# First expert by blocks of 128 tokens, its weights and rows gathered in another order, and narrow counting products in the first search

## The chip, the core and the metric

The kernel runs on one core of one Trainium2 chip. A core has five engines that run side by side and wait for each other through semaphores: TensorE (PE in the profile, its weight loads PEld), VectorE (DVE), ScalarE (ACT), GpSimd (POOL) and SyncE (SP), and DMA engines that move data between the chip's main memory (HBM), SBUF and, by way of the engines, PSUM. The metric is the device time of one execution in microseconds (us), as the median of several runs.

## The reference

The first half is a gated linear attention with a complex decay, the second a mixture of experts with a fixed capacity. Cut to what matters here:

```python
# attention -> x of 3072 tokens by 384 features
logits = x @ w_gate                      # 3072 x 8
order = np.argsort(-logits.flatten())
for idx in order:                        # greedy: best pair first
    tok, e = int(idx) // E, int(idx) % E
    if assigned[tok] >= 0 or counts[e] >= cap:   # cap = 3072 // 8 = 384
        continue
    assigned[tok] = e
    counts[e] += 1
for e in range(E):
    mask = assigned == e
    h = np.maximum(x[mask] @ w1[e], 0.0)         # 384 x 384 by 384 x 1024
    out[mask] = h @ w2[e]                        # 384 x 1024 by 1024 x 384
```

## The kernel before

The attention takes the first 252 us or so and is the same in both kernels. It leaves the rows `x` in HBM (`xd`) and the logits of all tokens in SBUF (`z.lg`, 128 partitions by 24 columns by 8 experts).

**The search.** `Router.find` finds which expert fills up next and at which logit. It narrows a threshold in five rounds. In each round VectorE compares all tokens with 32 candidate thresholds (`ind`, 128 x 24 x 32), TensorE counts the hits by expert (`cnt`, from `ind` and the one-hot choice `oh`), VectorE turns the counts into a flag `f`, and TensorE adds the chosen step to the threshold row `thr` in PSUM: once with `steps` (called S below) and once with `weight` and `fm` (called FM). S and FM write `thr`, which the comparison reads, so a round goes round the engines: compare, count, reduce, FM, compare. The count is made by six products, each of four token columns at once, so that a result lies in four diagonal blocks. For most experts VectorE adds the four blocks (`merge`: `cs` and `half`); for the first search (`BY_PE`) ScalarE copies the block to SBUF (`y`) and four more products against an identity add them (`gather`, tile `sm`). In the first search the comparison is made in two halves (`PARTS`).

When the search has closed (a product `cnt<-f,onesb`, called CLOSE below, and a product with `tri`, the running count over partitions), `eidx` names the rows of the expert's weights, and `Router.slots` works out which tokens go in which slot: VectorE makes one-hot tiles `o` and `rh`, six products give `cnt<-rh,o`, and four small operations write the row numbers `idx`.

**The gathers.** GpSimd issues indirect DMAs, all on one queue: `w1t` (one expert's w1, 1.57 MB), `w2t` (1.57 MB) and three of `xg` (128 token rows each, 0.2 MB). For experts in `W2_LATE` the rows go ahead of w2.

**The expert.** Rows are transposed on TensorE (`acc<-ident,xg`, nine 128 x 128), then come 24 products per w1 (8 column blocks by 3) and 24 per w2 (3 row blocks by 8). Experts 1 to 7 use split numbers: ScalarE rounds a tile to a high part (`w1h`, `w2h`, `xh`, `hh`), VectorE makes the low part (`w1l`, `w2l`, `xl`, `hl`), and each product is three fp32r matmuls of 384 columns: 144 per expert. Expert 0 (`WHOLE1`, `WHOLE2`) uses plain fp32, where a matmul shows as two records in the trace, and needs no split. For all experts the tokens are 384 columns wide, so the first product wants all three row blocks.

**The order.** Nothing is issued as the code is written. `experts` records every operation in a `Plan`; `rank` gives each a due time minus an offset by kind (the table `M_OFF`), and `in_order` (a list scheduler with fixed costs) writes out one static order for each engine. Each engine then runs its own list strictly in that order. The main products of expert e and the search for expert e+1 are interleaved in this way. Ahead of expert 0's first transpose TensorE runs `WARM` products of two constants (`acc<-ident,mask`).

## Time and profile before

| | us |
|---|---|
| median of 3 runs (545.6 to 547.11) | 545.8 |
| the profiled execution | 550.18 |
| its span, first to last instruction | 548.4 |
| PE busy / DVE busy in the span | 445.6 / 437.1 |
| first search: count of round 1 to CLOSE | 257.7 to 269.2 |
| first main product of expert 0 (w1) | 288.0 |
| CLOSE of the second search | 295.4 |
| last matmul | 540.5 |

The profiled execution took 550.18 us, 1.8 us more than its span and 4.4 us more than the median of the runs shown; differences within the span are read as differences of the median. Positions are in us from the start of the span. A "record" is one matmul instruction of the trace; matmuls overlap in the pipe, so the pitch between records, not the length of one, is what they cost.

### The profile page before, as it was taken

Reading aid. Unit: us, or ns where it says so; the run is one execution under the profiler, and the core shown is the slowest. Engines: PE = TensorE matmul, PEld = TensorE weight load, DVE = VectorE, ACT = ScalarE, POOL = GpSimd, SP = SyncE. Lnnn points to the kernel's source line nnn. Section 1 sums busy time; section 2 is a strip of 40 time slices with the busy share of each in tenths; the row PEclk is TensorE's granted clock in tenths of the full one; section 3 lists DMA queues with packets and bytes.
Section 4 is the critical chain, followed back from the end, with each engine's and each line's share of the span. In section 5 each row is a group of like instructions: output and inputs, shape, how many; then the busy total and the mean of one; then the engine's idle time right before and its main releaser. Section 6 shows DMA issues by size and latency. Waiting matters only on the chain. (4 is left out here: it accounts for less than half of the span.)

```text
span 548.4 us, 9215 instructions
## 1 busy us (share of the span) xinstructions
PE 445.6 (81%) x3383; PEld 392.6 (72%) x3383; DVE 437.1 (80%) x1267; ACT 276.5 (50%) x422; POOL 72.9 (13%) x87
## 2 busy tenths in 40 slices
PE   0005997699679967995489899999999999999994
PEld 0005996599678856994375458887889888999993
DVE  7999999979899989944667768889899898965240
ACT  5997579828887688322012513244172432834231
POOL 1000000000000000000121311332132223460102
PEclk9999999579859995998569999999999999999999
DMA  8625867578756885541071513245062431950001
GB/s 240 234 76 140 240 200 240 140 193 215 247 155 178 242 276 154 136 120 45 0 274 48 208 47 131 78 177 221 30 244 73 159 130 39 393 189 16 30 14 43
DMA packets 47596, 82.47 MB, mean 150 GB/s; under 512 B 5568, under 2 KB 43200, under 8 KB 45504
## 3 DMA queue, kind: packets, MB, share of 16 engines
q1 hardware_dynamic: 38720, 42.57, 27.2%
q0 software_dynamic: 5376, 34.61, 16.9%
q10 hardware_dynamic: 3456, 4.72, 2.5%
q8 instruction: 26, 0.43, 0.3%
q14 instruction: 18, 0.15, 0.1%
HBM read 53.49 MB, written 9.44 MB: 115 GB/s over the span
## 5 line engine op out<-in xcount | busy, mean ns | idle before, releaser
L131 PE MATMUL sc<-KQ 96*128 96x128 f32 x384 | 60.3, 317 | 41.6 <-DMA KQ<-f 40.7
L131 PEld LDWEIGHTS sc<-KQ 96*128 96x128 f32 x384 | 55.2, 226 | 44.0 <-DMA KQ<-f 41.6
L131 ACT ACTIVATE hh<-acc 128x384 fp32r<-128x384 f32 (+1 forms) x64 | 30.6, 490 | 75.2 <-PE acc L131 75.0
L131 PE MATMUL acc<-w2h,hl 128*128 128x384 f32 x168 | 55.1, 346 | 0.0
L131 PE MATMUL acc<-w2l,hh 128*128 128x384 f32 x168 | 54.9, 345 | 0.0
L131 PE MATMUL acc<-w2h,hh 128*128 128x384 f32 x168 | 54.4, 343 | 0.0
L131 PE MATMUL acc<-xh,w1h 128*128 128x384 f32 x168 | 53.6, 347 | 0.3 <-DVE idx L131 0.2
L131 PE MATMUL acc<-xl,w1h 128*128 128x384 f32 x168 | 53.1, 345 | 0.0
L131 PE MATMUL acc<-xh,w1l 128*128 128x384 f32 x168 | 52.6, 343 | 0.0
L131 POOL DMA_INDIRECT w1t<-in_w,eidx x8 | 8.8, 1099 | 312.4 <-DVE of L131 269.3
L131 ACT ACTIVATE ot<-acc 128x384 f32<-128x384 f32 x24 | 11.8, 492 | 70.7 <-PE acc L131 55.8
L131 DVE TENSOR_TENSOR f<-kq,CS 128x768 f32<-128x768 f32 x48 | 43.7, 949 | 0.9 <-ACT CS L131 0.9
L131 DVE SCALAR_TENSOR_TENSOR hl<-acc,hh 128x384 fp32r<-128x384 f32 x56 | 30.4, 551 | 15.9 <-ACT hh L131 15.3
L131 PE MATMUL y<-am,V 128*64 128x128 f32 x384 | 38.0, 288 | 3.0 <-DVE am L131 2.0
L131 DVE TENSOR_TENSOR ind<-m,thr 128x768 bf16<-128x768 f32 (+1 forms) x40 | 33.7, 849 | 6.9 <-PE thr L131 6.6
L131 PE MATMUL kp<-ident,KQ 96*128 96x96 f32 x160 | 25.0, 301 | 15.7 <-DMA KQ<-f 9.5
L131 POOL DMA_INDIRECT out<-ot,idx x24 | 25.3, 1053 | 93.2 <-ACT ot L131 82.9
L131 DVE TENSOR_TENSOR am<-sc,mask 128x512 f32<-128x512 f32 x48 | 31.5, 680 | 6.2 <-PE sc L131 6.1
L131 PE MATMUL U<-V,kt 128*96 128x96 f32 x320 | 35.2, 270 | 0.9 <-DVE tmp L131 0.9
L131 POOL DMA_INDIRECT xg<-xd,idx x24 | 28.1, 1172 | 57.1 <-DVE idx L131 29.4
L131 PEld LDWEIGHTS U<-V,kt 128*96 128x96 f32 x320 | 33.1, 184 | 2.7 <-issue 1.2
L131 PE MATMUL xp<-pick,xT 112*128 112x104 f32 x192 | 25.9, 285 | 10.7 <-ACT xT L131 8.5
(195 smaller groups left out, 1082.7 us busy)
## 6 DMA issues: line engine op xcount, KB each, us to landing
KQ<-f SPq DMA_DIRECT2D x192, 96.4 KB, 2.2
V<-in_v SPq DMA_DIRECT2D x8, 576.0 KB, 4.8
kq<-in_k SPq DMA_DIRECT2D x8, 576.0 KB, 6.6
kq<-in_q SPq DMA_DIRECT2D x8, 576.0 KB, 7.8
xd<-x ACTq DMA_DIRECT2D x24, 192.0 KB, 3.0
ai<-in_a_im SPq DMA_DIRECT2D x7, 576.0 KB, 4.4
ar<-in_a_re SPq DMA_DIRECT2D x7, 576.0 KB, 5.1
ai<-in_a_im SPq DMA_DIRECT2D x1, 384.0 KB, 3.6
```

The lines of the kernel that those rows point to most:

```text
L131: r = f(*a, **k)
```

## The change

Four things. First, in the first search (and in the slots of expert 0) the count is made by 24 products of one token column each, 32 stationary columns wide, that add up in one PSUM block; `gather` (ScalarE copy and four products) is gone; expert 6's slots, which also used it, get the narrow products too. Second, in every search S is issued after the counting products and no longer ahead of them. Third, the four `idx` operations are kept together. Fourth, expert 0 is computed by blocks of 128 tokens: transposes, w1 products (128 columns each, 72 in all) and w2 products block after block, its rows gathered ahead of its w2; `WARM` goes from 26 to 18. The offsets `M_OFF` are all new, so the static order moves everywhere from the first search on; the attention's part of each engine's list is unchanged.

```diff
     def find(self, parts, by_pe, more):
...
             both = ps.tile([128, 128], F32, name="cnt")
+            whole = both[:32, :E]
             for lot in range(0, NT, w):
                 with nc.one():
-                    if not lot:
-                        nc.tensor.matmul(thr, z.onesb[:2].to_broadcast([2, 128]), self.steps[:, it], start=False, stop=False, skip_group_check=True)
-                    for c in range(lot, lot + w, 4):
+                    for c in range(lot, lot + w) if by_pe else ():
+                        nc.tensor.matmul(whole, ind[:, c], oh[:, c], start=(c == 0), stop=(c == NT - 1))
+                    for c in range(lot, lot + w, 4) if not by_pe else ():
                         nc.tensor.matmul(both[:, :32], ind[:, c:c + 4].rearrange("p c j -> p (c j)"),
                                          oh[:, c:c + 4].rearrange("p c e -> p (c e)"), start=(c == 0), stop=(c == NT - 4))
+                    if lot + w == NT:
+                        nc.tensor.matmul(thr, z.onesb[:2].to_broadcast([2, 128]), self.steps[:, it], start=False, stop=False, skip_group_check=True)
             cnt = t("cs", [32, E])
             if by_pe:
-                whole = self.gather(both[:, :32], E)
                 v.tensor_tensor(cnt, whole, need[:32], op=OP.subtract)
...
     def slots(self, pi, by_pe):
...
-            for c in range(0, NT, 4):
+            for c in range(NT) if by_pe else ():
+                nc.tensor.matmul(both[:32, :24].rearrange("p (a k) -> p a k", a=2), o32[:, c], rh[:, c],
+                                 start=(c == 0), stop=(c == NT - 1))
...
-        for s in range(4):
-            v.scalar_tensor_tensor(idx[32 * s:32 * s + 32], ic[:, 1, s::4], 128.0, ic[:, 0, s::4],
-                                   op0=OP.mult, op1=OP.add)
+        with nc.one():
+            for s in range(4):
+                v.scalar_tensor_tensor(idx[32 * s:32 * s + 32], ic[:, 1, s::4], 128.0, ic[:, 0, s::4],
+                                       op0=OP.mult, op1=OP.add)
...
+    def first_expert(xg):
+
+        x0 = wp.tile([128, 3, 3, 128], F32, name="x0", bufs=1)
+        h0 = wp.tile([128, 3, FK, 128], F32, name="h0", bufs=1)
+
+        def turn(j):
+            xp = pm.tile([128, 3, 128], F32, name="acc", bufs=5)
+            for kk in range(3):
+                o = plan.tensor.transpose(xp[:, kk], xg[:, j, kk * 128:kk * 128 + 128], z.ident)
+                o.main, o.kind = True, "tp"
+            act(x0[:, j], xp, AF.Copy).kind = "x"
+
+        def hidden(j):
+            for f0 in range(0, FK, 3):
+                n = min(3, FK - f0)
+                hp = pm.tile([128, 3, 128], F32, name="acc", bufs=5)
+                for i in range(n):
+                    col = slice((f0 + i) * 128, (f0 + i) * 128 + 128)
+                    with plan.one():
+                        whole(hp[:, i], [(w1s[0][:, kk, col], x0[:, j][:, kk]) for kk in range(3)])
+                act(h0[:, j][:, f0:f0 + n], hp[:, :n], AF.Relu).kind = "h"
+
+        def last(j):
+            op = pm.tile([128, DM], F32, name="acc", bufs=5)
+            whole(op, [(h0[:, j][:, f], w2t[0][:, f]) for f in range(FK)])
+            write(0, j, op)
+        turn(0)
+        turn(1)
+        hidden(0)
+        turn(2)
+        hidden(1)
+        last(0)
+        hidden(2)
+        last(1)
+        return last
...
-    xs = tokens(0, xg)
...
+    xg0 = xg
+    xg = route(1)
+    last = first_expert(xg0)
+    xs = tokens(1, xg)
+    last(2)
...
-WARM = 26
+WARM = 18
...
-W2_LATE = (2,)
-WHOLE1 = (0,)
-WHOLE2 = (0,)
+W2_LATE = (0, 2)
```

Where the order moves. VectorE's list at the slots of expert 0, before (`ic` holds the counts of the slots, `idx` the row numbers; `cs`, `half`, `f` belong to the second search):

```order
L131 COPY ic<-sm 32x24
L131 SCALAR_TENSOR_TENSOR idx<-ic 32x3
L131 TENSOR_TENSOR cs<-cnt,need 32x8
L131 COPY half_2723<-cnt 32x8
L131 SCALAR_TENSOR_TENSOR idx<-ic 32x3
L131 TENSOR_TENSOR cs<-cs,cnt 32x8
L131 TENSOR_TENSOR half_2723<-half_2723,cnt 32x8
L131 SCALAR_TENSOR_TENSOR idx<-ic 32x3
L131 TENSOR_TENSOR cs<-cs,half_2723 32x8
L131 SCALAR_TENSOR_TENSOR idx<-ic 32x3
```

The same place in the changed kernel:

```order
L131 TENSOR_TENSOR ind<-m,thr 128x768
L131 TENSOR_TENSOR home<-home,tie 128x24
L131 COPY ic<-cnt 32x24
L131 SCALAR_TENSOR_TENSOR idx<-ic 32x3 x4
L131 TENSOR_TENSOR cs<-cnt,need 32x8
L131 COPY half_2792<-cnt 32x8
```

The four `idx` now stand together, ahead of the second search's counts. GpSimd's list of gathers from the first expert on, before:

```order
L131 DMA w1t<-in_w,eidx 128x3072
L131 DMA w2t<-in_w,eidx 128x3072
L131 DMA xg<-xd,idx 128x384 x3
L131 DMA w1t<-in_w,eidx 128x3072
L131 DMA w2t<-in_w,eidx 128x3072
L131 DMA xg<-xd,idx 128x384 x3
L131 DMA out<-ot,idx 3072x384 x3
```

The same place in the changed kernel:

```order
L131 DMA w1t<-in_w,eidx 128x3072
L131 DMA xg<-xd,idx 128x384 x3
L131 DMA w2t<-in_w,eidx 128x3072
L131 DMA w1t<-in_w,eidx 128x3072
L131 DMA w2t<-in_w,eidx 128x3072
L131 DMA xg<-xd,idx 128x384 x2
L131 DMA out<-ot,idx 3072x384
L131 DMA xg<-xd,idx 128x384
L131 DMA out<-ot,idx 3072x384 x2
```

Expert 0's rows stand ahead of its w2, and for expert 1 a store of expert 0's output now stands between the second and the third row gather. TensorE's list at expert 0's first main product, before:

```order
L131 MATMUL acc<-ident,mask 128x128 x2
L131 MATMUL acc<-ident,xg 128x128 x7
L131 LDWEIGHTS weight
L131 MATMUL thr<-fm,weight 128x32
L131 MATMUL acc<-ident,xg 128x128 x2
L131 MATMUL acc<-xh,w1t 128x384 x2
```

The same place in the changed kernel:

```order
L131 MATMUL acc<-ident,mask 128x128 x2
L131 MATMUL acc<-ident,xg 128x128 x3
L131 MATMUL acc<-ident,mask 128x128 x2
L131 LDWEIGHTS weight
L131 MATMUL thr<-fm,weight 128x32
L131 MATMUL acc<-ident,xg 128x128 x3
L131 MATMUL acc<-x_2841,w1t 128x128 x6
```

The first w1 products stand behind six transposes instead of nine, and one round earlier of the second search: the FM shown is that of its third round before, of its second round now.

## Rows read from the trace of the kernel before

**Rows 1.** Windows: length; PE, PEld, DVE, ACT, POOL busy (x instructions); clock, DMA share, GB/s.

```profile
295.40:331.80 36.40, 34.19 (x149) 19.26 (x149) 27.08 (x112) 12.26 (x24) 9.34 (x8) 0.95 0.31 114
363.50:396.10 32.60, 31.49 (x204) 27.24 (x204) 29.86 (x119) 12.75 (x26) 8.12 (x8) 1.00 0.36 134
540.50:548.40 7.90, 0.00 (x0) 0.00 (x0) 0.00 (x0) 0.49 (x1) 0.97 (x1) 0.82 0.07 25
```

**Rows 2.** Windows, PE records into `acc` alone (transposes and main products).

```profile
286.70:295.40 8.70, 8.13 (x29) 1.00 0.00 1
295.40:331.80 36.40, 32.41 (x97) 0.95 0.31 114
363.50:396.10 32.60, 29.54 (x152) 1.00 0.36 134
461.80:540.50 78.70, 77.42 (x445) 1.00 0.31 118
```

**Rows 3.** Timeline, one round of the first search: start, length, engine, instruction, [idle before].

```profile
259.06 1.02 DVE L131 TENSOR_TENSOR ind<-m,thr 128x384 bf16<-128x384 f32 x2 [0.19 <-PE thr L131]
...
260.24 0.34 PE L131 MATMUL cnt<-oh,ind 128*128 128x32 bf16 x6
...
260.87 0.25 PE L131 MATMUL sm<-y,ident 128*32 128x8 f16 x4 [0.28 <-ACT y L131]
...
261.16 0.15 DVE L131 TENSOR_SCALAR_CACHE_REDUCE f<-sm 32x8 bf16<-32x8 f32 x1 [1.08 <-PE sm L131]
...
261.59 1.02 DVE L131 TENSOR_TENSOR ind<-m,thr 128x384 bf16<-128x384 f32 x2 [0.19 <-PE thr L131]
```

**Rows 4.** Timeline, slots of expert 0: products, copy, last row number, first row gather.

```profile
276.45 0.66 PE L131 MATMUL cnt<-rh,o 128*128 128x96 bf16 x6 [3.14 <-DVE rh L131]
...
277.92 0.17 DVE L131 COPY ic<-sm 32x24 f32<-32x24 f32 x1
...
279.64 0.16 DVE L131 SCALAR_TENSOR_TENSOR idx<-ic 32x3 int32<-32x3 f32 x1
...
280.07 0.95 POOL L131 DMA_INDIRECT xg<-xd,idx  x1 [5.22 <-DVE f L131]
```

**Rows 5.** DMA, 272 to 290 us in 40 slices of 0.45 us: GB/s.

```profile
GB/s 0 0 0 0 0 218 109 273 328 437 437 437 437 437 437 437 382 437 437 410 446 410 315 277 222 273 242 160 236 89 27 7 0 0 0 0 0 0 0 0
```

**Rows 6.** Timeline of PE: warming products, then expert 0's w1 products.

```profile
280.25 2.50 PE L131 MATMUL acc<-ident,mask 128*128 128x128 f32 x10
...
282.99 1.58 PE L131 MATMUL acc<-ident,mask 128*128 128x128 f32 x12
...
284.62 1.38 PE L131 MATMUL acc<-ident,mask 128*128 128x128 f32 x10
...
287.99 1.46 PE L131 MATMUL acc<-xh,w1t 128*128 128x384 f32 x4
...
297.87 6.05 PE L131 MATMUL acc<-xh,w1t 128*128 128x384 f32 x18
```

**Rows 7.** Timeline, a later row gather (expert 3): issue of its first block.

```profile
375.29 0.97 POOL L131 DMA_INDIRECT xg<-xd,idx  x1 [5.91 <-DVE idx L131]
```

**Rows 8.** DMA, 375 to 381 us in 40 slices of 0.15 us: GB/s.

```profile
GB/s 410 0 430 676 143 154 355 225 133 41 0 0 0 246 123 215 236 277 154 62 0 154 92 184 236 348 236 62 0 0 246 184 61 225 317 195 82 0 0 0
```

**Rows 9.** Timeline, expert 1's gathers and a wait of PE in the second stretch.

```profile
297.52 1.04 POOL L131 DMA_INDIRECT w1t<-in_w,eidx  x1 [13.99 <-DVE open L131]
...
306.40 1.06 ACT L131 ACTIVATE w1h<-w1t 128x1024 fp32r<-128x1024 f32 x1 [3.24 <-DMA w1t<-in_w,eidx]
...
310.85 1.21 DVE L131 TENSOR_TENSOR w1l<-w1t,w1h 128x1024 fp32r<-128x1024 f32 x1
311.66 2.31 POOL L131 DMA_INDIRECT xg<-xd,idx  x1 [0.30 <-issue]
...
312.73 0.17 PE L131 MATMUL thr<-fm,weight 32*128 32x32 bf16 x1 [2.21 <-DVE f L131]
```

**Rows 10.** Windows by the level of TensorE's clock (columns as in Rows 1).

```profile
255.50:282.80 27.30, 13.07 (x110) 11.01 (x109) 18.07 (x91) 1.77 (x7) 4.20 (x5) 0.50 0.30 117
...
313.50:316.90 3.40, 3.40 (x13) 1.57 (x12) 2.83 (x9) 0.00 (x0) 1.61 (x2) 0.50 0.40 109
```

More of the change, by code (lines that the diff above doesn't have):

```diff
@@ L747, in keys @@
         self.quantize(self.key, self.z.lg)
-    def gather(self, x, n):
-        nc, z = self.nc, self.z
-        y = self.wk.tile(x.shape, F16, name=f"y{n}")
-        nc.scalar.activation(y, x, AF.Copy)
-        o = self.ps.tile([32, 32], F32, name="sm")[:, :n]
-        with nc.one():
-            for c in range(4):
-                nc.tensor.matmul(o, z.ident16[:, 32 * c:32 * c + 32], y[:, n * c:n * c + n], start=(c == 0), stop=(c == 3))
-        return o
     def find(self, parts, by_pe, more):
@@ L948, in slots @@
         with nc.one():
-            for c in range(0, NT, 4):
+            for c in range(NT) if by_pe else ():
+                nc.tensor.matmul(both[:32, :24].rearrange("p (a k) -> p a k", a=2), o32[:, c], rh[:, c],
+                                 start=(c == 0), stop=(c == NT - 1))
+            for c in range(0, NT, 4) if not by_pe else ():
                 nc.tensor.matmul(both[:, :96], o32[:, c:c + 4].rearrange("p c j -> p (c j)"),
@@ L1241, in route @@
             w1s[e] = pair([128, 3, FF], "w1", 2)
-        for kk in range(3) if e not in WHOLE1 else ():
-            split(w1t[:, kk], *(w[:, kk] for w in w1s[e]), "w1s", g if (e, kk) in W1_POOL else v)
+            for kk in range(3):
+                split(w1t[:, kk], *(w[:, kk] for w in w1s[e]), "w1s", g if (e, kk) in W1_POOL else v)
         plan.kind = f"next{e}"
@@ L1249, in route, with write, issue @@
         return xg
+    def write(e, j, op):
+        ot = wk.tile([128, DM], F32, name="ot")
+        act(ot, op, AF.Copy).kind = "ot"
+        def issue(ot=ot, ix=idx[e][:, j:j + 1]):
+            s = nc.gpsimd.indirect_dma_start(
+                out=out, out_offset=bass.IndirectOffsetOnAxis(ap=ix.real(), axis=0), in_=ot.real(), in_offset=None)
+            for o in scat:
+                tc.declare_no_dep(s.ins, o.ins, reason="other rows")
+            scat.append(s)
+        move(issue, [], [ot, idx[e][:, j:j + 1]], 128 * DM * 4, "out")
+    def first_expert(xg):
[3 more added lines that the diff above has]
+            xp = pm.tile([128, 3, 128], F32, name="acc", bufs=5)
+            for kk in range(3):
+                o = plan.tensor.transpose(xp[:, kk], xg[:, j, kk * 128:kk * 128 + 128], z.ident)
[23 more added lines that the diff above has]
+        return last
     def tokens(e, xg):
-        xs = pair([128, 3, CAP], "x", 1) if e not in WHOLE1 else wp.tile([128, 3, CAP], F32R, name="xh", bufs=1)
+        xs = pair([128, 3, CAP], "x", 1)
         for kk in range(3):
@@ L1269, in experts @@
         o.deps.append(router.placed)
-    xs = tokens(0, xg)
-    for e in range(E):
-        whole2 = e in WHOLE2
-        w2s = pair([128, FK, DM], "w2", 1) if not whole2 else None
-        hs = pair([128, FK, CAP], "h", 1) if not whole2 else wp.tile([128, FK, CAP], F32R, name="hh", bufs=1)
+    xg0 = xg
[3 more added lines that the diff above has]
+    last(2)
+    for e in range(1, E):
+        w2s = pair([128, FK, DM], "w2", 1)
+        hs = pair([128, FK, CAP], "h", 1)
         if e < E - 1:
@@ L1279, in experts @@
             col = slice(f * 128, f * 128 + 128)
[L1280 to L1286 removed]
+            product(hp, [([w[:, kk, col] for w in w1s[e]], [x[:, kk] for x in xs]) for kk in range(3)], True)
             hi, lo = (h[:, f] for h in hs)
@@ L1293, in experts @@
             row = slice(j * 128, j * 128 + 128)
-            if whole2:
-                whole(op, [(hs[:, f, row].bitcast(F32), w2t[e][:, f]) for f in range(FK)])
-            else:
-                product(op, [([h[:, f, row] for h in hs], [w[:, f] for w in w2s]) for f in range(FK)])
-            ot = wk.tile([128, DM], F32, name="ot")
-            act(ot, op, AF.Copy).kind = "ot"
-            def issue(ot=ot, ix=idx[e][:, j:j + 1]):
-                s = nc.gpsimd.indirect_dma_start(
-                    out=out, out_offset=bass.IndirectOffsetOnAxis(ap=ix.real(), axis=0), in_=ot.real(), in_offset=None)
-                for o in scat:
-                    tc.declare_no_dep(s.ins, o.ins, reason="other rows")
-                scat.append(s)
-            move(issue, [], [ot, idx[e][:, j:j + 1]], 128 * DM * 4, "out")
+            product(op, [([h[:, f, row] for h in hs], [w[:, f] for w in w2s]) for f in range(FK)])
+            write(e, j, op)
             if j == 1 and e < E - 1:
```

18 lines of the change are left out of this document (4 added, 14 removed).

## The prediction

> **What bounds the kernel now.** I read the page first, then windows over the second half, then the timeline of its first 45 us. Up to 252 us both kernels are the same. From there the program falls into three parts. Until 288 us TensorE has no main work: the first search and its slots pass from engine to engine, then the rows must arrive. From 288 to 540.5 us TensorE is hardly ever free: in the last stretch, 461.8 to 540.5, it is busy with main records alone for 77.42 of 78.7 us, 445 records at 0.174 us [rows 2]. After its end only 7.9 us of stores follow [rows 1], which the change doesn't touch. So what counts is when TensorE gets its first main product and what it loses on the way.
>
> What it loses: the order of before puts 143 split records and 9 transposes into 363.5 to 396.1 us [rows 2], 143 x 0.174 + 9 x 0.1 = 25.8 us, so 6.8 of 32.6 us go to the search's products and to waits. In 295.4 to 331.8 there are 76 fp32 records, 12 split ones and 9 transposes. An fp32 record of 384 columns costs (6.05 - 1.46)/(18 - 4) = 0.33 us [rows 6], so 76 x 0.33 + 12 x 0.174 + 0.9 = 28.1 and 8.3 us are lost. There TensorE waits 2.21 us for a flag of the search [rows 9] and then runs 3.4 us at the lower clock, 1.2 GHz [rows 10], some 1.5 us of delay. VectorE is nearly as full: 29.86 of 32.6 us [rows 1]. It is what TensorE's waits wait for, and it is why I don't count on the whole lead surviving.
>
> **The change, part by part.**
>
> *First search.* Now: the two half-comparisons end at 260.08, six count products run from 260.24 to 260.58, ScalarE copies, four products run to 261.12, and the flag starts at 261.16 [rows 3]; a round takes 261.59 - 259.06 = 2.53 us. In the change the first twelve narrow products run under the second half-comparison, since S no longer stands before them. The last twelve start about 0.1 us after it. Their pitch: four products of 32 stationary columns and 8 moving ones take 0.25 us [rows 3]; taking off one product's latency, about 0.17, leaves 3 steps of 0.027. So they end at 260.08 + 0.1 + 12 x 0.027 + 0.15 = 260.65, and the flag moves from 261.16 to about 260.7: 0.5 us a round, **2.5 us** for five. It would be 2.0 if the pitch were double.
>
> The Trainium skill speaks against this: TensorE: Matmul & The Clock Gate (section "Wait — 56ns, not 53.3ns?") gives a floor of about 25 ns between the starts of small matmuls, but about 62 ns where the sequencer decodes them itself. With 62 ns the last twelve would take 0.74 us and a round would save 0.1 us, the search 0.5. The trace's 27 ns agrees with the lower floor.
>
> *Slots of expert 0.* ScalarE's copy and four products go, 18 narrow products come. `ic` can start when VectorE has done `oh`, `tie`, the 0.87 us comparison and `home`, only 0.2 us earlier than now. But the four `idx` then stand together: now 279.64 + 0.16 - 277.92 = 1.9 us from `ic` to the last [rows 4], then about 0.9. Together 1.2 us. The first row gather moves from 280.07 [rows 4] to 280.07 - 2.5 - 1.2 = **276.4**.
>
> *Rows before w2.* Now the rows queue behind both weight gathers on one queue: the transfers run at up to 440 GB/s from 274.3 to about 286 us [rows 5], and the first transpose starts at 286.7 though the rows were issued by 283.5. Without weights ahead of them three row gathers go out 1.27 us apart and each is over some 2.7 us after its issue [rows 7, 8]. In the change w1 goes alone and 2.5 us earlier, and is done by about 276. The rows land at 279.1, 280.4 and 281.6; w2 is issued at 280.2 and is needed only after 291. Not the rows but TensorE's own list is now last: after the slots it holds ten warming products (20 records) around the first flag, the second count, and two more products. At the low clock a warming record takes 0.25 us (2.50/10), at the high one 0.10 ((1.58 - 1.38)/2) [rows 6]. The clock was low until 282.8 [rows 10], with TensorE dense since the slots' products at 276.45 [rows 4]; in the change those come 2.5 us earlier. If it rises at 279 to 280, the first w1 product starts at 281.3; if only at 282.8, at 283.4. I take 282.0 against 287.99 [rows 6]: **6.0 us earlier** (4.6 to 6.7).
>
> *What is still to do then.* Three transposes more (0.3) and one more round of the second search among main work (0.45). The w1 products: 72 x 2 records of 128 columns against 24 x 2 of 384. At 0.11 that is 15.8 us against 15.8: nothing. If weight loads showed through (1.38/10 = 0.14), it would be 4 us more; the difference between the two warm rows, at the same size and with a weight load each, speaks for 0.10 to 0.11. So a lead of **5.2 us**.
>
> *The second stretch (second to third search).* The old wait of 2.21 and the cold 3.4 us go: 3.5 us. New waits come. VectorE's list has `idx`, then `w1l`, then the counts; `w1l` wants ScalarE's `w1h`, and that wants w1, which here landed 8.9 us after its issue, with w2 right behind it (297.52 to 306.40) [rows 9]. I count 1.5 us there. And expert 1's third row gather now stands behind a store, while its transposes have moved forward: by the new order 6.9 us of main records and about 1 us of the search stand between the slots' products and the third row block's transpose, against 17 before. From those products it is 2.2 us to the last `idx` and the issue, three issues of 1.27 us (the store is one), and 2.7 to land: 8.7, so 0.8 us of wait. Together 2.3 to 3 us new against 3.5 old: **0.5 us gained** (from 2 gained to 3 lost).
>
> *The other stretches.* The main work in each is 22.6 to 26 us by the new order, 25.3 to 26.9 by the old, with the same sum from the second search on but for what is already done. S behind the count lets each of 30 counts start 0.11 us earlier; that helps only where TensorE would wait for the flag: **0.5 us gained** (0 to 3). The last search and `rest` now stand within 20 + 6 + 15 records of main work in place of 28 + 8 + 22: I count **0.7 us lost**. The rest of the new order I take as even, within 2 us either way.
>
> Sum: 5.2 + 0.5 + 0.5 - 0.7 = 5.5 us. On the profiled execution that is 550.2 - 5.5 = 544.7; on the median, 4.4 us below the profiled time, 545.8 - 5.5 = **540.3 us**.
>
> **The rivals.** (a) *The lead is lost in the second stretch*: no measurable change. The third rows of expert 1 come later than counted, because an issue of a row gather takes 2.31 us beside VectorE's splits [rows 9] where others take 0.97 [rows 7]. Two such issues cost 2.2 us more; with the 0.8 that is a wait of 3 us, and if the clock falls again as it did after 2.21 us [rows 9, 10], 1.5 us more. That undoes 4.0 of the 5.5: 544.3. The Trainium skill has a reason for such issues: GPSIMD Engine Reference (section "1. Specifications") says that GpSimd shares its SBUF interfaces with VectorE and contends with instructions that read two SBUF inputs. By that rule the two issues beside `w1l` would be slow again; the trace agrees, since the 2.31 us issue begins beside `w1l` (310.85 to 312.06) [rows 9].
>
> (b) *More comes through*: VectorE's chain was the pace, so the earlier counts and the kept-together `idx` shorten every stretch by 0.7 us, and the clock rises early: 5.5 + 0.7 + 5 x 0.7 = 9.7, so 536.1.
>
> (c) *Slower*: the clock stays low into expert 0. There are 8 warming products fewer, and the product blocks are broken by transposes and by waits for the second search. The 78 records of w1 before CLOSE take 8.6 us at the high clock and 17 at the low one. It decides if the low clock lasts 7 us or more beyond the first w1 product; the whole 8.4 us would give 548.7. Against it: the clock rose here within 6.5 us of dense work and stayed up but for one fall.
>
> (d) *No change at all* is not open: w2 is behind the rows, and nothing else held the rows.
>
> **How the numbers follow.** About 0.3%, 1.6 us, is what a measurement of this kernel tells from no change. Forecast, 536.5 to 543.5: 0.64. Rival (a), 543.5 to 547: 0.14. Rival (b), 534 to 536.5: 0.12. Rival (c) or the new order's own waits, above 547: 0.10. Faster (below 544.2) are the forecast, (b) and a little of (a): 0.77. Same: 0.13. Slower: 0.10. The range 535.5 to 545.5 leaves out (c), the far side of (b) and the upper part of (a), about 2 in 10.
>
> **What would show it.** Rounds of 2.0 to 2.1 us in the first search; the first row gather near 276.4; the first w1 product at 281 to 283.5, with the clock already or soon at 2.4 GHz; CLOSE of the second search near 292; a pitch of 0.11 us for the w1 records; w2 landed before it is wanted; in the second stretch no wait above 2 us and no fall of the clock; the last matmul near 535. The prediction is wrong if the first w1 product starts after 285, if the w1 records cost 0.14, if the third rows of expert 1 hold TensorE for over 2 us, or if the later stretches grow by a microsecond each.

## The result, and the profile after

The changed kernel took 544.24 us (median of 12 executions, 542.29 to 546.73), the kernel before, run beside it, 547.86 us (12 executions, 545.6 to 549.77). The ratio is 0.9944, 95% interval 0.9924 to 0.9963: a gain of 3.1 us by the ratio and 3.6 by the medians, where 5.5 were forecast. The profiled execution of the change took 542.76 us, 7.4 us less than the 550.18 of the profile that the prediction was read from. So the two profiles lie further apart than the kernels do, and that gap is what the experiments had to explain.

First what was forecast. The timeline of one round of the first search in the changed kernel (columns as in [rows 3]):

```profile
262.84 1.02 DVE L131 TENSOR_TENSOR ind<-m,thr 128x384 bf16<-128x384 f32 x2 [0.19 <-PE thr L131]
263.45 0.95 PE L131 MATMUL cnt<-oh,ind 128*32 128x8 bf16 x24 [0.65 <-DVE ind L131]
264.33 0.20 PE L131 MATMUL thr<-steps,onesb 2*128 2x32 bf16 x1
264.44 0.15 DVE L131 TENSOR_SCALAR_CACHE_REDUCE f<-cnt 32x8 bf16<-32x8 f32 x1 [0.57 <-PE cnt L131]
...
264.87 0.55 DVE L131 TENSOR_TENSOR ind<-m,thr 128x384 bf16<-128x384 f32 x1 [0.20 <-PE thr L131]
```

The 24 narrow products start at 263.45, while the second half-comparison still runs, and a round is 264.87 - 262.84 = 2.03 us against 2.53 [rows 3]. Then the slots, expert 0's gathers and the start of its products, from the timelines of VectorE, POOL and TensorE:

```profile
275.34 0.66 DVE L131 SCALAR_TENSOR_TENSOR idx<-ic 32x3 int32<-32x3 f32 x4
...
276.27 0.96 POOL L131 DMA_INDIRECT xg<-xd,idx  x1 [5.17 <-DVE cs L131]
...
280.04 0.95 POOL L131 DMA_INDIRECT w2t<-in_w,eidx  x1 [0.30 <-issue]
...
282.67 1.50 PE L131 MATMUL acc<-x,w1t 128*128 128x128 f32 x12
```

The first row gather goes out at 276.27 (forecast 276.4; before 280.07, [rows 4]), the first w1 product starts at 282.67 (forecast 282.0; before 287.99, [rows 6]). Twelve w1 records of 128 columns end 1.50 us after the start of the first; four records of 384 columns, which are as many columns, took 1.46 [rows 6]. Windows by the clock's level, and the second stretch, between CLOSE of the second and of the third search (columns as in [rows 1]):

```profile
256.28:280.17 23.89, 14.91 (x193) 12.43 (x194) 17.46 (x89) 0.53 (x1) 4.10 (x5) 0.50 0.25 83
280.17:536.20 256.03, 247.99 (x1606) 222.09 (x1604) 192.96 (x731) 96.46 (x197) 70.72 (x60) 1.00 0.35 129
...
294.06:327.74 33.68, 31.69 (x191) 22.36 (x191) 26.94 (x111) 12.27 (x24) 9.86 (x8) 1.00 0.35 127
```

TensorE's clock was at 1.2 GHz for 23.89 us (27.3 before, [rows 10]) and then at 2.4 GHz to the end, without the fall of [rows 10]. The second stretch is 33.68 us where [rows 1] had 36.40. By its profile alone the prediction came true, and more than true. The timed executions say that this profile, or the one before, or both, are not the usual case.

### The profile page after: what moved, and what is told of

Read it like the earlier page. It is cut to its first block, busy times and chain, and to the rows that moved or that the text cites. A ratio compares the mean times of both kernels' runs of the same rounds, so it can differ in the third digit from the quotient of the medians.

```text
span 541.0 us, 9559 instructions
## 1 busy us (share of the span) xinstructions
PE 442.9 (82%) x3561; PEld 400.9 (74%) x3561; DVE 436.1 (81%) x1267; ACT 275.8 (51%) x416; POOL 77.4 (14%) x87
## 4 chain that ended last, share of the span: by engine, by line
PE 50%; DVE 22%; issue 9%; DMA 7%; ACT 7%; POOL 2%; SPq 1%; POOLq 0%; ACTq 0%; DVEq 0%
PE acc L131 30%; PE sc L131 5%; PE y L131 4%; DVE f L131 4%; PE U L131 4%; DMA xd<-x 3%; DVE neg L131 3%; DVE zi L131 3%; DMA ar<-in_a_re 3%; ACT s L131 2%; PE cnt L131 2%; PE xp L131 2%; PE kp L131 2%; DVE kq L131 1%; DVE hl L131 1%
## 5 line engine op out<-in xcount | busy, mean ns | idle before, releaser
L131 ACT ACTIVATE hh<-acc 128x384 fp32r<-128x384 f32 x56 | 27.4, 492 | 63.3 <-PE acc L131 63.1
L131 PE MATMUL acc<-w2h,hl 128*128 128x384 f32 x168 | 53.4, 343 | 0.0
L131 PE MATMUL acc<-xl,w1h 128*128 128x384 f32 x168 | 51.4, 344 | 0.0
L131 PE MATMUL acc<-xh,w1h 128*128 128x384 f32 x168 | 51.3, 345 | 0.0
L131 PE MATMUL acc<-xh,w1l 128*128 128x384 f32 x168 | 51.1, 343 | 0.0
L131 POOL DMA_INDIRECT out<-ot,idx x24 | 31.7, 1322 | 110.9 <-ACT ot L131 101.3
L131 DVE TENSOR_TENSOR ind<-m,thr 128x768 bf16<-128x768 f32 (+1 forms) x40 | 33.7, 848 | 5.9 <-PE thr L131 5.6
L131 DVE TENSOR_TENSOR am<-sc,mask 128x512 f32<-128x512 f32 x48 | 31.5, 680 | 6.3 <-PE sc L131 6.2
L131 PE MATMUL xp<-pick,xT 112*128 112x104 f32 x192 | 25.9, 285 | 12.8 <-ACT xT L131 11.5
L131 PE MATMUL U<-V,kt 128*96 128x96 f32 x320 | 34.6, 267 | 0.9 <-DVE tmp L131 0.9
L131 PEld LDWEIGHTS kp<-ident,KQ 96*128 96x128 f32 x160 | 19.9, 173 | 19.9 <-DMA KQ<-f 10.8
L131 PEld LDWEIGHTS xp<-pick,xT 112*128 112x128 f32 x192 | 23.6, 197 | 14.7 <-ACT xT L131 12.2
```

Source lines behind the costliest of these rows:

```text
L131: r = f(*a, **k)
```

## The experiments

Sixteen runs were made in four groups (e1 to e4, e5 to e8, e9 to e12, e13 to e16), each group on one chip beside the kernel before; every ratio is to that. "Held" below means that the order of all instructions was taken from the unedited kernel and only the named ones moved. Where an edit changes costs instead, the planner orders much of the later program anew.

### Both kernels again

Unchanged copies, the kernel before twice and the changed one three times.

> The kernel before, unchanged. Theory A (the executions scatter, and the two profiled ones lie at opposite ends): the ratio is 1.000 within 0.002, but this profile lies 2 to 5 us below the first one's 550.2, and differs from it in named places: the 3.4 us at the lower clock at 313.5 us and the 2.21 us wait ahead of it are absent or shorter, and the end of TensorE's main work comes at 536 to 538.5 in place of 540.5. Theory B (the profiles are typical and 7.4 us is the true gain of an undisturbed execution; the timed runs hide it by something else): the profile is again 549 to 551 with the same wait and the same fall of the clock.

> The changed kernel, unchanged. Theory A (scatter): ratio 0.993 to 0.996, a profile of 543.5 to 546 with the same place for the first w1 product (282.7 within 0.5 us, counted from the end of attention) and 1 to 3 us more spread over later stretches (issues of row gathers, waits for the search). Theory B (typical): ratio 0.986 to 0.990 and a profile of 542 to 543.

> The changed kernel, unchanged, beside the other three on one chip. Theory A: ratio 0.994 to 0.995; the profile is either like the first (issues 0.95 and 1.0, second stretch 33.7 us) or like the second (1.8 and 2.0, two waits of some 2.2 us in all, the clock falls, 36.0 us), more likely the second. Theory B: ratio below 0.992, as if the earlier 0.5% were scatter.

> The kernel before, unchanged, on the same chip. Ratio 1.000 within 0.002; a third profile of its second stretch: 34 to 36.5 us, with a wait of 1.5 to 2.2 us for the flag if expert 1's w1 lands late (8 us or more after its issue), 33.1 and no wait if it lands within 7.5 us.

> The changed kernel, unchanged, on the same chip. Ratio 0.992 to 0.9955; the profile has slow row issues (1.8 and 2.0 us) and waits of some 2.2 us for the third rows if w1 lands before idx, so that w1l begins right behind idx; issues of 0.95 to 1.0 if w1 lands later. Second stretch 34.5 or 36.0 us in the first case, 33.7 in the second.

Measured: the change 0.9947 (0.9926 to 0.9969), 0.9897 (0.9866 to 0.9927) and 0.9931 (0.9907 to 0.9955); the kernel before 0.9985 (0.9963 to 1.0007) and 0.9996 (0.9977 to 1.0015). The third timing of the change (e12) missed its expectation on the side of theory B, and its profile is neither of the two expected: slow issues, but a stretch of 34.5 us and no fall of the clock. The profile of e2, 547.41 us, lies above what either theory had. Weighted by the inverse squares of their intervals, the four timings of the change give 0.9935, 0.9924 to 0.9947: 3.6 us, 2.9 to 4.2. They lie somewhat further apart than their own intervals suggest, so this interval is rather too narrow.

Stage lengths in us from the seven profiles (starts of TensorE's records; as the end of attention stands the product `sm<-ident,mm`, which prepares the first search, 254.16 in the first profile of before and 254.44 in that of the change):

| | before: first, e1, e14 | changed: first, e2, e12, e15 |
|---|---|---|
| end of attention to CLOSE | 15.1, 15.1, 15.4 | 12.4, 12.6, 12.7, 12.4 |
| CLOSE to first row gather | 10.8, 10.8, 10.8 | 9.5, 9.4, 9.5, 9.4 |
| row gather to first w1 product | 7.9, 8.4, 8.5 | 6.4, 6.3, 5.4, 6.3 |
| to CLOSE of the second search | 7.5, 7.5, 7.5 | 11.4, 11.5, 11.4, 11.5 |
| second stretch | 36.3, 34.1, 33.1 | 33.7, 36.0, 34.5, 34.5 |
| next four stretches | 130.0, 129.7, 129.9 | 125.2, 125.2, 125.2, 125.3 |
| last CLOSE to the last product | 78.7, 78.5, 78.7 | 80.1, 80.9, 80.1, 81.1 |
| sum | 286.3, 284.1, 283.9 | 278.6, 281.9, 278.7, 280.5 |

Four of the seven rows repeat within 0.3 us. The start of w1 and the last row scatter by up to 1 us, the second stretch by 3.2 us in the kernel before and by 2.3 in the changed one. The end of attention scatters too (252.7 to 257.0 us over all profiles, in a part that no edit touches), which is why single totals say so little.

In the second profile of the change POOL, VectorE, ScalarE and TensorE stand like this in the second stretch (timeline, columns as in [rows 9]; the last line is a window, columns as in [rows 1]):

```profile
297.70 1.04 POOL L131 DMA_INDIRECT w1t<-in_w,eidx  x1 [15.13 <-DVE open L131]
304.58 1.06 ACT L131 ACTIVATE w1h<-w1t 128x1024 fp32r<-128x1024 f32 x1 [1.09 <-DMA w1t<-in_w,eidx]
306.25 0.66 DVE L131 SCALAR_TENSOR_TENSOR idx<-ic 32x3 int32<-32x3 f32 x4
306.93 1.23 DVE L131 TENSOR_TENSOR w1l<-w1t,w1h 128x1024 fp32r<-128x1024 f32 x1
307.17 1.81 POOL L131 DMA_INDIRECT xg<-xd,idx  x1 [7.19 <-DVE idx L131]
309.23 1.21 DVE L131 TENSOR_TENSOR w1l<-w1t,w1h 128x1024 fp32r<-128x1024 f32 x1
309.29 1.98 POOL L131 DMA_INDIRECT xg<-xd,idx  x1 [0.30 <-issue]
313.06 0.97 POOL L131 DMA_INDIRECT xg<-xd,idx  x1 [0.30 <-issue]
313.41 0.33 PE L131 MATMUL acc<-ident,xg 128*128 128x128 f32 x1 [0.52 <-DMA xg<-xd,idx]
316.15 0.33 PE L131 MATMUL acc<-ident,xg 128*128 128x128 f32 x1 [1.65 <-DMA xg<-xd,idx]
...
317.39:320.80 3.41, 3.41 (x15) 1.83 (x14) 1.99 (x4) 0.49 (x1) 0.00 (x0) 0.50 0.00 0
```

and in the first profile of the change like this:

```profile
296.14 1.04 POOL L131 DMA_INDIRECT w1t<-in_w,eidx  x1 [15.15 <-DVE open L131]
304.73 1.06 ACT L131 ACTIVATE w1h<-w1t 128x1024 fp32r<-128x1024 f32 x1 [2.81 <-DMA w1t<-in_w,eidx]
...
305.61 0.95 POOL L131 DMA_INDIRECT xg<-xd,idx  x1 [7.19 <-DVE idx L131]
305.82 1.23 DVE L131 TENSOR_TENSOR w1l<-w1t,w1h 128x1024 fp32r<-128x1024 f32 x1 [0.49 <-ACT w1h L131]
306.86 1.01 POOL L131 DMA_INDIRECT xg<-xd,idx  x1 [0.30 <-issue]
...
310.50 1.12 POOL L131 DMA_INDIRECT xg<-xd,idx  x1 [0.30 <-issue]
313.82 0.33 PE L131 MATMUL acc<-ident,xg 128*128 128x128 f32 x1 [1.18 <-DMA xg<-xd,idx]
```

In both, what differs is when w1 of expert 1 lands, read here from when ScalarE can start `w1h`. In the first profile of the change ScalarE could start w1h 304.73 - 296.14 = 8.6 us after w1's issue, so w1l wasn't ready when `idx` was, the first row issue began ahead of it and took 0.95 us. In the second it was 6.9 us; w1l followed `idx` at once, the two issues began beside it and took 1.81 and 1.98 us, and TensorE waited 0.52 and 1.65 us for the rows; then its clock fell to 1.2 GHz for 3.41 us at 317.4. Five profiles have the changed kernel's order up to there (e7, below, is the fifth): four have 1.8 and 2.0 us issues, with w1 6.9 to 7.6 us after its issue.

In the kernel before the same landing works the other way. There VectorE's list has w1l ahead of the third search's flag, so a late w1 makes TensorE wait: 2.21 us and a fall of the clock with w1 8.88 us after its issue [rows 9, 10], 1.49 us and no fall with 8.16 us (e1): 0.72 us later, and 0.72 us more of wait. In e14 it was 6.9 us. Timeline:

```profile
297.77 1.04 POOL L131 DMA_INDIRECT w1t<-in_w,eidx  x1 [14.62 <-DVE open L131]
304.71 1.06 ACT L131 ACTIVATE w1h<-w1t 128x1024 fp32r<-128x1024 f32 x1 [1.30 <-DMA w1t<-in_w,eidx]
...
308.07 1.81 POOL L131 DMA_INDIRECT xg<-xd,idx  x1 [8.02 <-DVE idx L131]
310.19 2.31 POOL L131 DMA_INDIRECT xg<-xd,idx  x1 [0.30 <-issue]
311.25 0.17 PE L131 MATMUL thr<-fm,weight 32*128 32x32 bf16 x1 [0.49 <-DVE f L131]
```

The row issues are slow as in the changed kernel, but no transpose waits for them, and the flag costs TensorE 0.49 us. The stretch is 33.1 us, as in e3 and e4 below, which have the same order there. So the first two profiles happened to have a late w1 both, which is the bad case of before and, by this one profile, the good one of the change. That is why they lie so far apart: their second stretches differ by 2.6 us (36.3 and 33.7), the means of the table by 0.2 the other way. Over all 18 profiles `w1h` starts 6.9 to 7.9 us after the issue of w1 in fifteen, and 8.16 us or more in three: the first of either kernel, and e1.

### Clearing the second stretch

The order is held. First the third row gather of expert 1 ahead of expert 0's first store (POOL alone):

```diff
 xg<-xd,idx  (expert 1, rows 0 to 127)
 xg<-xd,idx  (rows 128 to 255)
-out<-ot,idx (expert 0, first store)
 xg<-xd,idx  (rows 256 to 383)
+out<-ot,idx (expert 0, first store)
```

> The changed kernel with one POOL instruction moved: expert 1's third row gather is issued ahead of expert 0's first store; every other engine's list is as in the changed kernel. Theory A (the lead is given back in the second stretch: in the second profile of the changed kernel two row issues of 1.81 and 1.97 us beside VectorE's w1l, and the store's 1.19 us between, put the third rows at about 316, TensorE waits 0.52 and 1.65 us and its clock falls for 3.4 us, so the stretch is 36.0 us long; in the first profile the issues were 0.95 and 1.01 and it was 33.7): without the store in between the third rows come 1.5 to 2 us earlier, the wait goes, the clock stays, the stretch is 32 to 33.3 us, and the ratio to before falls from 0.9945 to 0.990 to 0.992. Theory B (the two microseconds that the timed executions lack are scatter of what lies ahead of the experts, or lie in later stretches): the stretch is shorter by at most 1.2 us, and the ratio stays at 0.993 to 0.996.

Then also expert 1's first two w1l moved behind the next comparison and behind the second flag (e6), and with two w2l put out of the way of the next comparison (e11, and e16 on another chip). The third search compares in one piece of 768 columns; the expectations call it a half-comparison.

```diff
 idx
-w1l
 cs ... f
-w1l
 ind
+w1l
 w2l w2l cs ... f
+w1l
```

> As the run before, and VectorE's first two w1l of expert 1 each moved a step later (behind the next half-comparison of the third search, and behind its second flag), so that they don't run beside the row issues nor ahead of the first flag. Their products start only at 320 us. Theory A: the first two row issues are 0.95 to 1.1 us, the flag's wait of 0.8 us at 308 goes, the stretch is 31 to 32.5 us, ratio 0.988 to 0.991. Rival (an issue's length has another cause than VectorE's w1l): the issues stay at 1.8 us or more, and the ratio is that of the run before.

> As with the third rows first and w1l later, but the second w1l stands in the place of two w2l (which go behind the third w1l), so that the next half-comparison isn't held up: there the run before waited 1.12 us. Theory A: three issues of 0.95, no wait over 0.6 us in the second stretch, which is 31.9 to 32.6 us long, no fall of the clock; ratio 0.988 to 0.990, the best so far. Rival (the stretch is as long, since VectorE has as much to do in it): 33.0 to 33.3 us and ratio 0.991.

> The changed kernel with the second stretch cleared (third rows ahead of the store, w1l later), on the same chip. Second stretch 33.0 to 33.2 us in every profile. If that stretch is the cause: ratio 0.988 to 0.991, 1.5 to 2.5 us below the change as it is. If not: within 0.7 us of it.

And the kernel before with its three w1l behind later comparisons or flags of the third search (held):

```diff
-idx w1l cs ... idx w1l cs ... w1l cs w2l f w2l ind
+idx cs ... idx cs ... cs w2l f w2l ind w1l
 w2l w2l cs ... f w2l ind
+w1l
 cs ... f
+w1l
```

> Before, with expert 1's three w1l on VectorE each moved behind a later half-comparison or flag of the third search; all other lists stay. If before's wait of 1.5 to 2.2 us in the second stretch comes from VectorE standing at w1l with the flag behind it, the wait is gone, row issues are 0.95 to 1.1 us, the stretch is 32.8 to 33.2 us in place of 34.1 to 36.3, and the ratio is 0.995 to 0.998. If not: 0.999 to 1.001.

Measured:

| run | ratio, interval | issues of the rows, us | second stretch, us |
|---|---|---|---|
| e5, third rows first | 0.9915 (0.9891 to 0.9939) | 1.81, 1.97, 1.14 | 33.2 |
| e6, w1l later too | 0.9909 (0.9876 to 0.9942) | 0.95, 0.95, 0.95 | 33.1 |
| e11, and two w2l | 0.9895 (0.9868 to 0.9923) | 0.95, 0.95, 0.95 | 33.1 |
| e16, as e11 | 0.9914 (0.9885 to 0.9942) | 0.95, 0.95, 0.95 | 34.0 |
| e13, before with w1l later | 1.0012 (0.9993 to 1.0031) | 0.95, 0.95, 1.30 | 33.9 |

The four cleared forms, weighted as above, give 0.9909, 0.9895 to 0.9922: 5.0 us. Against 0.9935 they are 1.5 us (0.5 to 2.4) better than the change as it is, but the two means come in part from different chips. Chip by chip, by the means of the executions, e11 is 0.35 us (1.50 either way) below e12, e16 0.67 us (1.03) below e15, and e5 and e6 together are 1.94 us (1.10) below e7, which has the change's second stretch. Weighted together that is 1.1 us, 0.4 to 1.8: the clearing gains, but how much is not well known.

Clearing the kernel before gains nothing in e13, which missed both its ratio and its stretch. It is a weak counterpart: w1 landed early there (7.4 us), and with a wait of 0.78 us for a flag its stretch is longer than the 33.1 us of the unedited order in e14.

POOL and VectorE in e11:

```profile
303.26 0.66 DVE L131 SCALAR_TENSOR_TENSOR idx<-ic 32x3 int32<-32x3 f32 x4
304.18 0.95 POOL L131 DMA_INDIRECT xg<-xd,idx  x1 [7.19 <-DVE cs L131]
305.44 0.95 POOL L131 DMA_INDIRECT xg<-xd,idx  x1 [0.30 <-issue]
306.69 0.95 POOL L131 DMA_INDIRECT xg<-xd,idx  x1 [0.30 <-issue]
307.04 1.22 DVE L131 TENSOR_TENSOR w1l<-w1t,w1h 128x1024 fp32r<-128x1024 f32 x1
307.94 1.18 POOL L131 DMA_INDIRECT out<-ot,idx  x1 [0.30 <-ACT w2h L131]
```

Without w1l ahead of them the same three issues take 0.95 us each, so the rival of e6 (another cause for their length) is out. But in e5 the issues are as slow as ever, and the stretch is 33.2 us all the same, since the third rows are issued 4.4 us after the first in place of 5.9. POOL and TensorE in e5:

```profile
310.99 1.14 POOL L131 DMA_INDIRECT xg<-xd,idx  x1 [0.30 <-issue]
...
312.88 0.33 PE L131 MATMUL acc<-ident,xg 128*128 128x128 f32 x1 [0.56 <-DMA xg<-xd,idx]
```

So by these few profiles slow issues alone (e5) cost 0.1 us against the 33.1 of e6 and e11, the store ahead of the third rows alone (first profile of the change) 0.6, both together 1.4 (e12, e15), and 2.9 where the clock falls too (e2, e7).

TensorE waits 0.73 us for a comparison at 319 in e11, 1.12 at 314.7 in e6, 1.20 for a flag at 315.5 in e16. With that the stretches are longer than expected: 33.1 us where e6 and e11 had 31 to 32.6, 34.0 where e16 had 33.0 to 33.2. VectorE is busy for 26.7 of 33.1 us in e11, and what doesn't wait for rows waits for it.

### The parts of the lead

S put back ahead of each count, in all searches; all lists but TensorE's stay, and that one but for S:

```diff
                 with nc.one():
+                    if not lot:
+                        nc.tensor.matmul(thr, z.onesb[:2]...)    # S
                     for c in range(lot, lot + w) if by_pe else ():
                         nc.tensor.matmul(whole, ind[:, c], oh[:, c], ...)
...
-                    if lot + w == NT:
-                        nc.tensor.matmul(thr, z.onesb[:2]...)    # S
```

> The changed kernel with S put back ahead of its count in all 35 rounds; VectorE's, ScalarE's and POOL's lists stay as they are, and TensorE's but for S. From the runs so far: with S ahead and narrow products a round of the first search took 2.45 us, with S behind 2.03, without narrow products 2.53 to 2.59. Theory C (S behind is worth 2 us, because the first twelve narrow products then run under the second half-comparison): rounds 2.45, CLOSE of the first search 14.4 us after the end of attention in place of 12.4 to 12.6, first w1 product 1.5 to 2 us later, ratio 0.997 to 0.999. My prediction's split (narrow products 2.5 us, S behind 0.5 us in the later searches only) would have rounds of 2.1 and a ratio of 0.9955.

The narrow products in the kernel before, S still ahead, and the same with `idx` together and expert 0's rows ahead of w2 (`W2_LATE = (0, 2)`); here the planner orders the later program anew:

```diff
-                whole = self.gather(both[:, :32], E)
+                    for c in range(lot, lot + w) if by_pe else ():
+                        nc.tensor.matmul(whole, ind[:, c], oh[:, c], start=(c == 0), stop=(c == NT - 1))
...
-W2_LATE = (2,)
+W2_LATE = (0, 2)
```

> Before, with the narrow products for the first search's counts and expert 0's slots, S still ahead of the count, idx not kept together, gathers in the old order. My steps: 0.4 to 0.5 us a round, 2.0 to 2.5 us in the search, some 0.2 in the slots; w1, w2 and the rows all move by that much, so 2.2 to 2.7 us at the first w1 product, and ratio 0.9955 if it comes through. The Trainium skill's other pitch (62 ns) would give 0.5 us: ratio 0.999. Rival (the lead is lost in the second stretch, where the flag and the third rows hold TensorE): first w1 product 2.5 us earlier but ratio 0.999 to 1.001. The order of the later stretches shifts with this edit too, which may hide or add a microsecond.

> Before, with the narrow products, expert 0's idx kept together and its rows ahead of w2, but expert 0 by 384 columns, 22 warming products, S ahead of the counts and the old offsets. My steps: the search 2.5 us and the slots 1.2 us earlier, rows landed by 282; the warming list and nine transposes then hold the first w1 product at 283.5 to 284.5 (3.5 to 4.5 us earlier than 288 to 289). Theory A (what is lost is lost in the new second stretch): this keeps it, ratio 0.9925 to 0.9945, as good as the whole change. Rival (blocks of 128 and the new offsets are worth microseconds): ratio 0.996 to 0.998.

Measured: e9 0.9949 (0.9925 to 0.9973) on the chip on which the change gave 0.9897, by the means 3.0 us (1.4 either way) more than e12; e4 1.0002 (0.9976 to 1.0028); e8 0.9979 (0.9957 to 1.0000). A round of the first search in e9, timeline:

```profile
264.32 1.02 DVE L131 TENSOR_TENSOR ind<-m,thr 128x384 bf16<-128x384 f32 x2 [0.19 <-PE thr L131]
265.39 0.18 PE L131 MATMUL thr<-steps,onesb 2*128 2x32 bf16 x1 [1.11 <-DVE ind L131]
265.50 0.80 PE L131 MATMUL cnt<-oh,ind 128*32 128x8 bf16 x24
...
266.77 1.02 DVE L131 TENSOR_TENSOR ind<-m,thr 128x384 bf16<-128x384 f32 x2 [0.20 <-PE thr L131]
```

S writes `thr`, so it waits for both half-comparisons that read it, and the first twelve products wait behind S: 2.45 us a round. So S behind the count is worth 0.42 us a round with the narrow products, and the narrow products alone some 0.1, which theory C said; S behind the count of the old wide products was not run. The end of attention to CLOSE is 14.8 us in e9 and 14.5 in e4 and e8. In the later searches S's place is worth nothing: the stretches from the third search on are 30.0, 32.0, 31.5 and 31.8 us in e9, 29.9, 32.0, 31.5 and 31.7 in e12.

In e8 the first w1 product comes 32.7 us after the end of attention, only 1.1 to 2.1 us earlier than in before, where 3.5 to 4.5 were expected: the expectations of e4 and e8 had lost sight of S, which the prediction names. e4 missed as well. Its first w1 product comes 32.1 us after the end of attention, 1.7 to 2.6 us earlier than in before, its last stretch is 79.9 us, 1.2 longer, and the timing shows no gain. (Its slots take 9.6 us like those of e8, since the planner put the four `idx` together there too.)

With the old blocks, old warming list and S ahead, e8 has 1.1 us (0 to 2.4) of the change's gain. That is what its rival expected, by which the blocks of 128 and the new offsets are worth microseconds. But S accounts for it: 3.6 us less the 3.0 of e9 leave 0.6 for the change with S ahead. So the timings show no gain from the blocks, the shorter warming list and the new offsets together, within some 1.5 us.

The order of expert 0's gathers, first in the kernel before (e3, by `W2_LATE = (0, 2)` alone), then (e7, held) put back in the changed one:

```diff
 w1t<-in_w,eidx
+w2t<-in_w,eidx
 xg<-xd,idx  (three)
-w2t<-in_w,eidx
```

> Before, with expert 0's rows fetched ahead of its w2 and nothing else. My steps: the rows land some 3 us earlier (282.8 to 285.5 in place of about 286.5), but TensorE's own list (22 warming products, to 286.0) then stands ahead of the transposes, so the first w1 product moves from 287.99 to 287.2 only: 0.5 to 0.9 us, ratio 0.9985. Rival (the rows are the whole lead, as the transfers' order alone decides): 2 to 3 us, ratio 0.995. Second rival (w2 comes too late for expert 0's second product, at 306 us): slower.

> The changed kernel with one POOL instruction moved: expert 0's w2 gather is issued right behind w1, ahead of the three row gathers; all other lists as they are. My steps: the rows then queue behind both weight gathers, which are through some 12 us after w1's issue, so they land at about 283 to 284.5 in place of 279.3 to 281.9 and the first w1 product starts 1.5 to 3 us later (284.5 to 285.5): ratio 0.998 to 1.000. Rival (the rows don't wait for the weights; TensorE's warming products and clock set the start): the first w1 product within 0.5 us of 282.7, ratio 0.9945 as with the change.

Measured: e3 0.9985 (0.9966 to 1.0005), and its first w1 product comes 34.6 us after the end of attention, no earlier than in before (33.8 to 34.8), where 0.5 to 0.9 were expected. e7 has 0.9938 (0.9913 to 0.9964), the same as with the change whole, so its rival holds. TensorE there (timeline)

```profile
281.23 0.71 PE L131 MATMUL acc<-ident,mask 128*128 128x128 f32 x4
282.58 0.55 PE L131 MATMUL acc<-ident,xg 128*128 128x128 f32 x3 [0.64 <-DMA xg<-xd,idx]
...
284.00 1.50 PE L131 MATMUL acc<-x,w1t 128*128 128x128 f32 x12
```

waits 0.64 us for rows that stand behind both weights; its first w1 product comes 28.4 us after the end of attention, against 27.5 to 28.3 with the rows first. The order w1, rows, w2 moves nothing that is waited for, since TensorE's own list ends no earlier.

Eight warming products in place of 18 (held; the other ten are left out):

```diff
+    for o in [o for o in ops if o.kind == "warm"][8:]:
+        ops.remove(o)
```

> The changed kernel with 8 warming products in place of 18 (the last ten are left out, which computes nothing that is used; the other lists stay). In the changed kernel TensorE's list ends with the transposes at 281.3 and 282.3, while the rows land at 279.3 to 281.9. Theory D (TensorE's own list sets the start): the first transposes start at 280 to 280.5 and the first w1 product at 281.5, 1 us earlier, if the clock still rises at 280. Rival (the warming products pay for the clock): with ten products fewer the clock rises 2 to 4 us later, and the first records of w1 run at 0.22 us; the second CLOSE then comes at the same time or up to 2 us later. Ratio 0.993 to 0.996 by the first, 0.995 to 0.999 by the second.

Measured: 0.9906 (0.9879 to 0.9933), level with the change on that chip. Timeline of TensorE and windows by clock:

```profile
276.31 2.08 PE L131 MATMUL acc<-ident,mask 128*128 128x128 f32 x8
279.98 0.90 PE L131 MATMUL acc<-ident,xg 128*128 128x128 f32 x3
281.92 2.76 PE L131 MATMUL acc<-x,w1t 128*128 128x128 f32 x12
284.89 1.60 PE L131 MATMUL acc<-x,w1t 128*128 128x128 f32 x12
...
257.40:284.70 27.30, 17.59 (x215) 14.49 (x215) 18.80 (x95) 1.51 (x3) 4.90 (x5) 0.50 0.33 105
```

Both theories are half right, and they cancel: the first w1 product comes 26.9 us after the end of attention, 0.6 to 1.4 us earlier than with 18, but the clock stays at 1.2 GHz for 27.3 us in place of 23.9, and the first twelve records take 2.76 us in place of 1.50. CLOSE of the second search is 39.6 us after the end of attention, where the change has 38.9 to 39.8.

## Why the prediction was right in kind and wrong in size

The forecast of a gain was right, and 544.24 us lies inside the range; the size was 5.5 us and the timings say 3.6 (2.9 to 4.2), 3.1 in the first of them. The time is 3.9 us above the 540.3 forecast, and only 1.9 of these are the gain (5.5 against 3.6 by the medians). The other 2.1 are the base: 545.8 was the median of three executions, and that of the twelve beside the change is 547.86. So it is luck that the time falls on rival (a)'s 544.3. That figure is off in itself, too: the 0.8 us are in the forecast already, so 2.2 and 1.5 undo 3.7 us and not 4.0.

By its steps:

- *First search, 2.5 us*: right. 15.1 to 15.4 us became 12.4 to 12.7. The mechanism was the one given, S no longer ahead of the first twelve products (the expectation of e9 reads the prediction otherwise): 0.42 of the 0.5 us a round are S (e9). The low pitch holds: 24 narrow products end 0.80 us after the first's start in e9, (0.80 - 0.17)/23 = 0.027 us each. Of the two figures in the Trainium skill (TensorE: Matmul & The Clock Gate, section "Wait — 56ns, not 53.3ns?") this is the lower, about 25 ns; its 62 ns would put the 24 at some 1.6 us by an estimate from that page, and the trace shows 0.80.
- *Slots, 1.2 us*: right, 10.8 became 9.4 to 9.5.
- *Rows before w2, then TensorE's own list last; first w1 product 6.0 us earlier*: right in the sum, 34.3 to 28.05 us after the end of attention on the mean, 6.3 us. The order of the gathers has almost no part in it (e7). What there is beyond search and slots, some 2.2 us, I put down to a shorter list ahead of the first product and a clock that rises with it; e10 shows that a shorter list moves that product, but no run takes the two apart.
- *Transposes and one more round, 0.75 us lost*: some 1.3. From the first w1 product to CLOSE of the second search it is 4.0 us longer, of which 78 x 0.111 - 18 x 0.33 = 2.7 us are products done earlier.
- *w1 records of 128 columns, nothing*: right, twelve take 1.50 us and six, elsewhere in the timeline, 0.83, so (1.50 - 0.83)/6 = 0.11 us each.
- *The second stretch, 0.5 us gained*: **this is the step that failed**, in its first sentence: "The old wait of 2.21 and the cold 3.4 us go: 3.5 us." Three of the five profiles that have before's order there (e3, e4 and e14 of first, e1, e3, e4, e14) show neither, with 33.1 us. Beyond its products the stretch lost 8.3 us in the profile that I read, and 33.1 - 28.1 = 5.0 us where w1 lands early. (The trace has 78 fp32 and 9 split records there, where the prediction counts 76 and 12: 28.2 us in place of 28.1.) The new waits were nearly right: 2.3 to 3 us were forecast on top of 4.8 (8.3 less the 3.5), so 7.1 to 7.8; measured are 66 x 0.111 + 48 x 0.33 + 16 x 0.174 + 0.9 = 26.8 us of products and 6.9, 9.2, 7.7 and 7.7 us beyond. Against the early case of before that is a loss of some 3 us, not a gain of 0.5; against the mean of before's three profiles (34.5 us, 6.4 beyond) 1.5. Their kind differs from the forecast: not w1h that holds w1l, but rival (a), slow row issues beside w1l and the third rows late behind the store, in four of five profiles, with a fall of the clock in two of them.
- *S behind the later counts, 0.5*: nothing (e9).
- *Last search, 0.7 lost*: some 0.2. It is 1.9 us longer on the mean, with 436 - 426 = 10 records of 0.174 more in it.
- *The other stretches even within 2*: 1.7 us gained. The four are 4.7 us shorter, with 17 records (3.0 us) fewer.

With the means of the profiles the steps come to 6.3 - 1.3 - 1.5 + 1.7 - 0.2 = 5.0 us, and the sums of the table differ by 4.85. With w1 early in both kernels (33.1 us in before, 34.5 to 36.0 in the change) the second stretch takes some 3 us in place of 1.5, and 3.5 us are left, near the 3.6 of the timings. That early is the usual case is shown by fifteen of the 18 profiles and not by the timings. The cleared form of the change brings back 1.1 us chip by chip (1.5 over all groups) and clearing before brings none, which agrees with this reading. What stays open: how often w1 lands late in a timed execution, and whether the 0.9897 of the one group is scatter or that chip's own.

One sign was on the table: I took the sum against the profiled 550.2 us and noted that the median lay 4.4 us below. I carried that difference over as a constant. It was in part the very wait that I counted as a gain.

The Trainium skill's rule behind rival (a) (GPSIMD Engine Reference, section "1. Specifications": GpSimd shares its SBUF interfaces with VectorE and contends with its instructions of two SBUF inputs) agrees with these traces: 1.81 us beside w1l, 0.95 without.

## What to carry to other kernels

A wait in one profile that hangs on when a transfer lands is a draw, not a property: before a sum counts its end as a gain, compare the profile's own time with the timed ones, and ask what the stretch costs if the transfer lands 2 us earlier. A transfer that lands early can also hurt, when it lets a long vector operation in just ahead of a gather's issue, and more so when a store stands in the same queue ahead of the rows that are waited for. And an operation that reads what others write (here S on `thr`) belongs behind the work that doesn't need it: that one line was worth most of the search's gain, once the products were narrow.

## What the runs showed of the hardware

A row gather's issue that begins while w1l runs on VectorE ends about 0.82 us after it: w1l 306.93 + 1.23 = 308.16, issue to 308.98; in the kernel before w1l 309.31 to 310.54, issue 309.55 to 311.36. The issue of 2.31 us in [rows 9] fits this if the two w2l are counted in that follow w1l there without a gap (timeline of before):

```profile
312.06 0.54 DVE L131 TENSOR_TENSOR w2l<-w2t,w2h 128x384 fp32r<-128x384 f32 x1
...
312.60 0.54 DVE L131 TENSOR_TENSOR w2l<-w2t,w2h 128x384 fp32r<-128x384 f32 x1
```

They end at 313.14, the issue at 311.66 + 2.31 = 313.97. An issue that begins 0.2 us or more ahead of w1l keeps its 0.95 us though w1l overlaps most of it (305.61 and 305.82 in the first profile of the change). So in these traces only the beginning of an issue is held.

After a wait of 1.65 to 1.74 us for rows, at the same place in the program, TensorE's clock fell in three profiles (e2, e7, e10) and stayed up in three (e9, e12, e15); after 2.21 us in before it fell [rows 10], after 1.49 (e1) it didn't.
